# Waits for the loads of keys, queries and values put on attention's value matmuls, with gathers, low parts and one high part moved

## The chip, the core and the metric

The kernel runs on one core of a Trainium2 chip. The metric is the device time of one execution in microseconds (us). Before the change the median of three runs is 1334.23 us (1333.91 to 1335.32). TensorE does the matmuls, ScalarE the exponentials, VectorE and GpSimd the elementwise work, and SyncE issues most of the DMA loads and stores; each engine takes its instructions in the order of the program.

## What is computed

A gated mix of full attention and of a mixture of experts, for 2048 tokens of width 448, 16 heads of 28 and 8 experts of which each token uses two:

```python
def _A_ref(x, wqkv, wo):          # attention
    ...
    scores = jnp.einsum("bhqd,bhkd->bhqk", q, k) * scale
    p = _softmax(scores, axis=-1)
    o = jnp.einsum("bhqk,bhkd->bhqd", p, v)
    return (lambda x, *d: x.transpose(*d))(o, 0, 2, 1, 3).reshape(B, S, D) @ wo

def _B_ref(x, w_gate, w1, w2):    # experts
    ...
    for e in range(E):
        mask = (topk_idx == e)
        w = (gates * mask).sum(-1, keepdims=True)
        h = _silu(xf @ w1[e]) @ w2[e]
        out = out + w * h
    return out.reshape(B, S, D)

g = _sigmoid((x * gate_w).sum(-1, keepdims=True))
return g * _A_ref(x, A_wqkv, A_wo) + (1 - g) * _B_ref(x, B_w_gate, B_w1, B_w2)
```

## The kernel before

Matrix products keep their accuracy by splitting each float32 operand into a rounded high part and a low part (the rest); a product is then two or three matmuls. ScalarE, VectorE or GpSimd make the parts: a copy gives the high part, a subtraction the low part.

The program has four stages. First it projects x: tiles of x and pieces of the weight wv are split and multiplied into values, gate and logits (the split of wv is at L372 and L373, that of x at L390 and L392, the matmuls at L381); the tokens are sorted to the experts, and queries and keys are projected. Queries, keys (as high and low parts) and values go to DRAM. Second come the experts, to about 825 us, with the maxima of the scores beside them; each expert's rows are stored to DRAM (`ys_d`). Third is attention, 835 to 1292 us. Last, 16 tiles of the output projection.

Attention runs over 16 units; a unit is one group of four heads with 512 queries, u = 4 * group + quarter. Each unit has 8 pairs p of key tiles. The loop takes m = (u, p) in order; in each pass it issues the scores of the next pair (`score_passes`, L762: 24 matmuls in sets of four heads that run beside each other on four row groups), then the values of this pair (`values`, L1271: 32 matmuls into banks z0 and z1), then what lies beside (`beside`). The exponentials of a pair go to ScalarE (L1230, L1231, L1239, L1240). The last 160 columns of the eighth block are instead raised by `power`: GpSimd computes u (L1246), n (L1247) and g (L1248), then takes one entry of the list `due`, then computes e (L1251); VectorE turns g and e into P (L1253 to L1257). VectorE also copies scores out (X, L1232), accumulates the values (osb, L1279 and L1281) and divides by the row sums (`divide_half`, L1166, in pairs 2 and 3, by `rs`, which GpSimd's queue loads).

In `due` stand GpSimd's small DMAs: the row sums' way through DRAM, and the gathers of the experts' rows for the output tiles (`fetch_routed`, L1111: an indirect DMA from `ys_d` into b; the second of a tile adds). A gather is put there after pairs 4 and 6 of a unit.

The keys and values of a group are held in two halves of eight key tiles: K0 and V0 for pairs 0 to 3, K1 and V1 for pairs 4 to 7. In the last unit of a group, `beside` issues on SyncE the next group's K0 at pair 3, V0 at pair 4 and K1 at pair 6. `scores` issues the next unit's queries (Q) at pair 0. V1 is issued by `beside` at pair 0 of the new group's first unit, once its buffer is free. V1 is one DMA of 512 KB (L720); K0 and K1 are 12 DMAs each (L733, L736), Q is 12 (L748, L750). The matmul that first reads a loaded tile waits for its DMAs; where a matmul waits for several, TensorE gets a wait instruction more for each beyond the first.

In the last unit the first two output tiles are prepared: `split_o_high` at pairs 0 and 4, `split_o_low` (L186 and L187 in `split_xl`: low parts of three blocks, then of the half block) at pairs 2 and 7.

Of the kernel before, what the change touches and what calls it, by code (L numbers as in the profile page):

```python
# [9 lines left out]
F32 = mybir.dt.float32  # L10
# [41 lines left out]
KR = DH + 1  # L52
# [11 lines left out]
def tile_gated_mha_moe(ctx: ExitStack, tc: tile.TileContext, x, xe_, xT, wv, wqk, wo, w1, w2, out):  # L64
# [120 lines left out]
    def split_xl(pt, h, l, n):
        nc.vector.tensor_tensor(l, pt[:, 0:3, :n], h[:, 0:3].bitcast(F32), op=ALU.subtract)  # L186
        nc.vector.tensor_tensor(h[64:128, 3], pt[64:128, 3, :n], h[64:128, 3].bitcast(F32),  # L187
                                op=ALU.subtract)
# [98 lines left out]
    with ExitStack() as pa:  # L287
# [81 lines left out]
            split_x(xts[t].rearrange("p (b n) -> p b n", b=4), xh[:, :, ts], xl[:, :, ts], 128)  # L369

        def split_wv(b):
            nc.scalar.activation(wv_h[:, b], wv_r[:, b], AF.Copy)  # L372
# [15 lines left out]
        def split_xb(b, cs):  # L388
# [4 lines left out]
            else:  # L393
                nc.vector.tensor_tensor(xh[64:128, b, cs], xb[64:128], xh[64:128, b, cs].bitcast(F32),
                                        op=ALU.subtract)

        split_xb(0, slice(0, 128))
        split_wv(0)
        split_xb(0, slice(128, 512))
        for b in range(1, FIRST):  # L400
            split_xb(b, slice(0, 512))
# [313 lines left out]
    c0 = ctx.enter_context(tc.tile_pool(name="pc_sb0", bufs=1, side="right", reuse_waits="tile"))  # L715
    cpool = [c0, None]

    def load_v(g, hf):
        t = cpool[hf].tile([128, NT // 2, 128], F32, name=f"V{hf}")
        nc.sync.dma_start(t, v_d[hf * 1024:(hf + 1) * 1024, g * 128:(g + 1) * 128]  # L720
                          .rearrange("(t p) d -> p t d", p=128))
        return t


    def load_k(g, hf):
        r = []
        cs = slice(hf * 1024, (hf + 1) * 1024)
        for part, src in (("h", qkh_d), ("l", qkl_d)):
            kt_ = cpool[hf].tile([128, 1024], F32R, name=f"K{part}{hf}")
            kf = kt_.bitcast(F32)  # L730
            for j in range(4):
                r0 = D + (4 * g + j) * DH
                nc.sync.dma_start(kf[32 * j:32 * j + DH].rearrange("p (c n) -> p c n", c=2),  # L733
                                  src[2 * hf:2 * hf + 2, r0:r0 + DH].rearrange("c r n -> r c n"))
                if part == "h":
                    nc.sync.dma_start(kf[32 * j + DH:32 * j + KR], neg_d[:, cs])  # L736
            r.append(kt_)
        return r


    def load_q(g, qc):
        need_max(g, qc)
        q = c0.tile([128, 2, 512], F32R, name="Q", bufs=2)
        qf = q.bitcast(F32)
        for i, src in enumerate((qkh_d, qkl_d)):
            for j in range(4):
                r0 = (4 * g + j) * DH
                nc.sync.dma_start(qf[32 * j:32 * j + DH, i], src[qc, r0:r0 + DH])  # L748
        for j in range(4):
            nc.sync.dma_start(qf[32 * j + DH:32 * j + KR, 0], m_d[4 * g + qc, j:j + 1])  # L750
        return q

    Ps = {}
# [367 lines left out]
        else:  # L1121
            nc.vector.tensor_copy(oh, OT[:, :, t * 128:(t + 1) * 128])

    def split_o_low(t):
        split_xl(OT[:, :, t * 128:(t + 1) * 128], *halves[t], 128)

    def split_o(t, eng):
        split_o_high(t, eng)
# [70 lines left out]
    due = []  # L1199
# [18 lines left out]
    def scores(m):  # L1218
        u, p = divmod(m, NPR)
        if p == 0 and u and u + 1 < NU:  # L1220
            qs[u + 1] = load_q((u + 1) // 4, (u + 1) % 4)
        X = sb.tile([128, 512], F32, name="X")
        P = sb.tile([128, 8, 512], F32, name="P")
        z, t = [None] * 2, [None] * 2
        for i in range(2):
            kt = 2 * p + i
            z[i], t[i] = single(i), triple(i)
            three = [t[i][:, j] for j in range(3)]
            score_passes(kt, held[u // 4][0][kt // 8], qs[u], three + [z[i]] if i else [z[i]] + three)
        nc.scalar.activation(P[:, 0], z[0], AF.Exp, scale=SCALE)  # L1230
        nc.scalar.activation(P[:, 1:4], t[0], AF.Exp, scale=SCALE)  # L1231
        nc.vector.tensor_scalar(X, z[1], LAM * SCALE * math.log2(math.e), -126.0 * LAM, op0=ALU.mult, op1=ALU.max)  # L1232
# [6 lines left out]
        nc.scalar.activation(P[:, 4:7], t[1], AF.Exp, scale=SCALE)  # L1239
        nc.scalar.activation(P[:, 7, 0:512 - w], X[:, 0:512 - w], AF.Exp, scale=math.log(2.0) / LAM)  # L1240
        Pc[m] = [P[:, i] for i in range(8)]

    def power(x, to):
        u, n, g, y = (sb.tile([128, PW], F32, name=f"p{c}", bufs=1 + (c == "u")) for c in "ungy")
        e, v, w = u.bitcast(I32), x, g
        nc.gpsimd.tensor_scalar(u, x, 1.0 / LAM, ROUND, op0=ALU.mult, op1=ALU.add)  # L1246
        nc.gpsimd.tensor_scalar(n, u, -ROUND, LAM, op0=ALU.add, op1=ALU.mult)  # L1247
        nc.gpsimd.tensor_tensor(g, n, x, op=ALU.subtract)  # L1248
        if due:
            due.pop(0)()  # L1250
        nc.gpsimd.tensor_scalar(e, u, 127.0 - ROUND, 2.0 ** 23, op0=ALU.add, op1=ALU.mult)  # L1251
# [5 lines left out]
        nc.vector.scalar_tensor_tensor(to, w, EXP2[3], e.bitcast(F32), op0=ALU.add, op1=ALU.mult)  # L1257

    def values(m):
# [6 lines left out]
        for n, i in runs:  # L1266
            po, cs = parts[n]
            kt = 2 * p + i
            v = held[u // 4][1][kt // 8]
            for j in range(4):  # L1270
                nc.tensor.matmul(po[32 * j:32 * j + 32, cs], v[:, kt % 8, 32 * j:32 * j + 32], P[4 * i + j][:, cs],  # L1271
                                 start=i == 0, stop=i == 1)
# [14 lines left out]
    def beside(m):  # L1287
        u, p = divmod(m, NPR)
        g, qc = divmod(u, 4)
        if qc == 3 and g + 1 < NG:  # L1290
            if p == 3:
                held[g + 1] = [load_k(g + 1, 0), None], [None, None]
            if p == 4:
                held[g + 1][1][0] = load_v(g + 1, 0)
            if p == 6:
                held[g + 1][0][1] = load_k(g + 1, 1)
        if g and qc == 0 and p == 0:
            held[g][1][1] = load_v(g, 1)
# [18 lines left out]
        if u == NU - 1:  # L1317
            if p in (0, 4):
                split_o_high(p // 4, nc.vector)
            if p in (2, 7):  # L1320
                split_o_low(p // 7)

    for m in range(NU * NPR):
        if m + 1 < NU * NPR:
# [1 line left out]
        values(m)  # L1326
        u, p = divmod(m, NPR)
        if u + 1 < NU and p in (4, 6):
            due.append(lambda t=u + 1, c=p // 2 - 2: fetch_routed(t, c))
        if u == 0 and p in (0, 2):  # L1330
            due.append(lambda t=u, c=p // 2: fetch_routed(t, c))
        beside(m)
        if m + 1 in powers:
            next(powers[m + 1])
# [74 lines left out]
```

## Time and profile before

| | before |
|---|---|
| median of three runs | 1334.23 us |
| the profiled execution's own time | 1334.03 us |
| its span | 1332.2 us |
| TensorE busy | 1325.2 us |
| VectorE busy | 1064.0 us |
| GpSimd busy | 856.7 us |
| ScalarE busy | 843.5 us |
| granted TensorE clock | 1.00 |

The profile is of one execution. A row of a timeline has start and duration in us, the engine (PE is TensorE, PEld its weight loads, DVE VectorE, ACT ScalarE, POOL GpSimd, SPq SyncE's DMA queue), the line, the operation, out<-in and the number of instructions merged into it; in brackets stands an idle before it, with what ended it. A row of the windows has each engine's busy time in a stretch with the instructions in brackets, then the granted clock, the DMA engines' busy share and GB/s.

### The profile page before, as it was taken

The page shows a single profiled execution, that of the slowest core. Times are in us where ns is not written, and L with a number is a line of the kernel's source. Part 1 is how long each engine was busy: PE and PEld are TensorE (multiplying, and loading weights), DVE is VectorE, ACT ScalarE, POOL GpSimd, SP SyncE. Part 2 cuts the span into 40 slices and gives each one's busy share as a digit, 9 for nine tenths or more (in the row PEclk, how much of TensorE's full clock was granted, in tenths as well). Part 3 has the DMA queues.
Part 4 walks back from the last instruction along what each step waited for, and adds up shares of the span by engine and source line. Part 5 has one row for each costly group of instructions (what it writes and reads, how often), then busy time and mean ns, then how long its engine had stood idle before and what let it go on. Part 6 is the DMA issues. An engine that isn't in the chain of part 4 may idle for free. (4 is left out here: it accounts for less than half of the span.)

```text
span 1332.2 us, 32345 instructions
## 1 busy us (share of the span) xinstructions
PE 1325.2 (99%) x12210; PEld 936.9 (70%) x12210; DVE 1064.0 (80%) x1667; ACT 843.5 (63%) x1271; POOL 856.7 (64%) x1142
## 2 busy tenths in 40 slices
PE   9999999999999999999999999999999999999999
PEld 8888788788887777777777777555555555555558
DVE  5746899888898888989888786777788778777775
ACT  5325454355364344543445434999999999999981
POOL 2143967877787788786887844666666666656641
PEclk9999999999999999999999999999999999999999
DMA  9887657554553475455746423212422432242214
GB/s 349 301 268 267 185 162 187 153 151 109 166 157 86 149 203 149 137 125 155 187 120 184 93 78 68 62 39 64 121 54 70 113 81 49 76 111 54 49 41 137
DMA packets 139520, 176.83 MB, mean 133 GB/s; under 512 B 25576, under 2 KB 107242, under 8 KB 138850
## 3 DMA queue, kind: packets, MB, share of 16 engines
q1 hardware_dynamic: 120626, 145.68, 36.0%
q0 software_dynamic: 18592, 28.84, 10.5%
q8 instruction: 96, 1.57, 0.5%
q14 instruction: 62, 0.51, 0.1%
q10 hardware_dynamic: 144, 0.23, 0.1%
HBM read 124.54 MB, written 53.25 MB: 133 GB/s over the span
## 5 line engine op out<-in xcount | busy, mean ns | idle before, releaser
L149 DVE TENSOR_REDUCE mp<-pm 128x3 f32<-128x1536 f32 (+1 forms) x301 | 508.9, 1733 | 10.9 <-PE pm L128 10.8
L1271 PE MATMUL z<-P,V 128*32 128x288 f32 x4064 | 247.9, 382 | 1.0 <-ACT P L1230 0.2
L1271 PEld LDWEIGHTS z<-P,V 128*32 128x32 f32 x4064 | 110.2, 109 | 132.7 <-ACT P L1230 48.5
L1065 ACT ACTIVATE yo<-acc,cg 128x448 f32<-128x448 f32 x64 | 40.7, 636 | 232.1 <-PE acc L1050 222.7
L833 POOL TENSOR_TENSOR w2l<-w2r,w2h 128x448 fp32r<-128x448 f32 x112 | 130.6, 1167 | 86.1 <-ACT w2h L827 64.9
L762 PE MATMUL s<-Q,Kh 29*128 29x512 f32 x1524 | 185.7, 437 | 0.0
L1239 ACT ACTIVATE P<-s 128x1536 f32<-128x1536 f32 x127 | 185.4, 1460 | 0.0
L1231 ACT ACTIVATE P<-s 128x1536 f32<-128x1536 f32 x127 | 183.6, 1446 | 0.0
L762 PE MATMUL z<-Q,Kh 29*128 29x512 f32 x508 | 182.7, 438 | 0.0
L1050 PE MATMUL acc<-w2h,hh 128*128 128x448 f32 x448 | 167.0, 373 | 0.3 <-PEq L847 0.3
L1050 PE MATMUL acc<-w2h,hl 128*128 128x448 f32 x448 | 166.5, 372 | 0.0
L1050 PE MATMUL acc<-w2l,hh 128*128 128x448 f32 x448 | 166.1, 371 | 0.0
L997 ACT ACTIVATE hf<-acc 128x512 f32<-128x512 f32 (+6 forms) x154 | 74.3, 482 | 136.5 <-PE acc L993 130.6
L142 DVE TENSOR_REDUCE mp<-acc 128x1 f32<-128x512 f32 x130 | 89.5, 688 | 83.9 <-PE pm L128 81.8
L842 POOL TENSOR_TENSOR hl<-hf,hh 128x512 fp32r<-128x512 f32 x112 | 145.9, 1303 | 1.1 <-ACT hh L1000 0.5
L993 PE MATMUL acc<-xeh,w1h 128*128 128x512 f32 (+3 forms) x408 | 136.8, 339 | 0.0
L993 PE MATMUL acc<-xeh,w1l 128*128 128x512 f32 (+3 forms) x408 | 136.1, 338 | 0.0
L1246 POOL TENSOR_SCALAR pu<-X 128x160 f32<-128x160 f32 x126 | 44.4, 353 | 132.7 <-DVE X L1232 131.2
L1281 DVE TENSOR_TENSOR osb<-z,osb 128x288 f32<-128x288 f32 x224 | 95.1, 425 | 41.6 <-PE z L1271 31.9
L1232 DVE TENSOR_SCALAR X<-z 128x512 f32<-128x512 f32 x127 | 87.8, 691 | 44.5 <-PE z L762 30.8
L801 POOL TENSOR_TENSOR w1l<-w1r,w1h 128x1024 fp32r<-128x1024 f32 (+1 forms) x49 | 91.1, 1860 | 43.7 <-ACT w1h L795 24.2
L128 PE MATMUL pm<-khg,qg 28*128 28x512 f32 x894 | 110.5, 449 | 0.9 <-DVE lo L672 0.9
(238 smaller groups left out, 3072.4 us busy)
## 6 DMA issues: line engine op xcount, KB each, us to landing
w2r<-in_w_dram SPq DMA_DIRECT2D x112, 224.0 KB
w1r<-in_w_dram SPq DMA_DIRECT2D x56, 384.0 KB
x_d<-xf SPq DMA_DIRECT2D x115, 64.0 KB
ys_d<-zero_d SPq DMA_DIRECT2D x32, 224.0 KB
qkh_d<-hi SPq DMA_DIRECT2D x28, 256.0 KB
qkl_d<-lo SPq DMA_DIRECT2D x28, 256.0 KB
w1r<-in_w_dram SPq DMA_DIRECT2D x112, 64.0 KB
ys_d<-yo SPq DMA_DIRECT2D x32, 224.0 KB
```

Source lines behind the costliest of these rows:

```text
L128: nc.tensor.matmul(banks[n], qgs[g, qt // 4][rw, (qt % 4) * 128:(qt % 4 + 1) * 128], kh[g, kc][rw], start=True, stop=True)
L149: nc.vector.tensor_reduce(mp[:, (o + lo) % 256:(o + lo) % 256 + hi - lo], pm[h][:, lo - 3 * h:hi - 3 * h], axis=AX.X, op=ALU.max)
L762: nc.tensor.matmul(banks[j], k[rw, ks], q[rw, c], start=i == 0, stop=i == 2)
L801: nc.gpsimd.tensor_tensor(l[:, :, half], r[:, :, half], h[:, :, half].bitcast(F32), op=ALU.subtract)
L833: nc.gpsimd.tensor_tensor(w2l, w2r, w2h.bitcast(F32), op=ALU.subtract)
L842: nc.gpsimd.tensor_tensor(hl, hf32, hh[:, 0:512].bitcast(F32), op=ALU.subtract)
L993: nc.tensor.matmul(pu[:, 0:HC], a, b[:, cs], start=i == 0, stop=i == len(mms) - 1)
L1050: nc.tensor.matmul(py[:n, 0:D], a[:, cs], b, start=i == 0, stop=i == 3 * NH - 1)
L1231: nc.scalar.activation(P[:, 1:4], t[0], AF.Exp, scale=SCALE)
L1239: nc.scalar.activation(P[:, 4:7], t[1], AF.Exp, scale=SCALE)
L1271: nc.tensor.matmul(po[32 * j:32 * j + 32, cs], v[:, kt % 8, 32 * j:32 * j + 32], P[4 * i + j][:, cs], start=i == 0, stop=i == 1)
L1281: nc.vector.tensor_tensor(accs[u][:, cs], po[:, cs], accs[u][:, cs], op=ALU.add)
```

## The change

Four edits. (1) The gathers get a list of their own, `rows`, which is taken behind e instead of ahead of it. (2) In the last unit each low part is made in two pieces: the three blocks at pair 1 (first tile) and pair 5 (second), the half block at pairs 6 and 7. (3) The first high part of wv is copied by VectorE instead of ScalarE, and stands ahead of the first split of x. (4) The loads of K, Q and V are recorded, and `behind_values(u, p)` makes the value matmuls of pair (u, p) wait for those issued since the last such call, one DMA each, all but the first and the last of a block: Q at (u, 5), K0 at (u, 6), V0 at (u, 7), K1 at (u + 1, 1), V1 at (u, 2), where u is the unit that issues the load.

```diff
+            if b:
+                nc.scalar.activation(wv_h[:, b], wv_r[:, b], AF.Copy)
+            else:
+                nc.vector.tensor_copy(wv_h[:, b], wv_r[:, b])
...
+        split_wv(0)
         split_xb(0, slice(0, 128))
-        split_wv(0)
...
+    landing = []
+
+    def load(to, src):
+        landing.append(nc.sync.dma_start(to, src))
+
+    def landed():
+        r = landing[::-1]
+        landing.clear()
+        return r
...
+    def behind_values(u, p):
+        arrivals.setdefault(u * NPR + p, []).extend(landed())
...
             qs[u + 1] = load_q((u + 1) // 4, (u + 1) % 4)
+            behind_values(u, 5)
...
         nc.gpsimd.tensor_scalar(e, u, 127.0 - ROUND, 2.0 ** 23, op0=ALU.add, op1=ALU.mult)
+        if rows:
+            rows.pop(0)()
...
-                nc.tensor.matmul(po[32 * j:32 * j + 32, cs], v[:, kt % 8, 32 * j:32 * j + 32], P[4 * i + j][:, cs],
-                                 start=i == 0, stop=i == 1)
+                mm = nc.tensor.matmul(po[32 * j:32 * j + 32, cs], v[:, kt % 8, 32 * j:32 * j + 32],
+                                      P[4 * i + j][:, cs], start=i == 0, stop=i == 1)
+                if arrivals.get(m) and (i, j) not in ((0, 0), (1, 3)):
+                    tc.add_manual_dep(mm.ins, arrivals[m].pop(0).ins.name, DATA, reason="operands' arrival")
...
                 held[g + 1] = [load_k(g + 1, 0), None], [None, None]
+                behind_values(u, 6)
...
                 held[g + 1][1][0] = load_v(g + 1, 0)
+                behind_values(u, 7)
...
                 held[g + 1][0][1] = load_k(g + 1, 1)
+                behind_values(u + 1, 1)
         if g and qc == 0 and p == 0:
             held[g][1][1] = load_v(g, 1)
+            behind_values(u, 2)
...
-            if p in (2, 7):
-                split_o_low(p // 7)
+            if p in (1, 5):
+                split_o_low(p // 5, 0)
+            if p in (6, 7):
+                split_o_low(p - 6, 1)
...
-            due.append(lambda t=u + 1, c=p // 2 - 2: fetch_routed(t, c))
+            rows.append(lambda t=u + 1, c=p // 2 - 2: fetch_routed(t, c))
```

On TensorE, in unit 4, these are the value matmuls of pair 2 and the first scores of pair 4, which are the first to read K1; DMAHW3 and the like are semaphores of SyncE's loads. Before:

```order
L1271 MATMUL z0_12267<-P_12156,V0_11845 32x288 [waits Activation_49]
L1271 MATMUL z0_12267<-P_12156,V0_11845 32x288 x7
L1271 MATMUL z1_12268<-P_12156,V0_11845 32x224 [waits DVE_49]
L1271 MATMUL z1_12268<-P_12156,V0_11845 32x224 x6
L1271 MATMUL z1_12268<-P_12156,V0_11845 32x224 [waits DVE_49]
L762 MATMUL z0_12293<-Q_11406,Kh1_11985 128x512 [waits DMAHW4_49,DMAHW3_49,DVE_49]
L762 MATMUL s0_12294<-Q_11406,Kh1_11985 128x512 [waits DMAHW6_49,DMAHW5_49,Activation_49]
L762 MATMUL s0_12294<-Q_11406,Kh1_11985 128x512 [waits DMAHW7_49,DMAHW0_49]
L762 MATMUL s0_12294<-Q_11406,Kh1_11985 128x512 [waits DMAHW2_49,DMAHW1_49]
```

And after:

```order
L1296 MATMUL z0_12267<-P_12156,V0_11845 32x288 [waits Activation_49]
L1296 MATMUL z0_12267<-P_12156,V0_11845 32x288 [waits DMAHW3_49]
L1296 MATMUL z0_12267<-P_12156,V0_11845 32x288 x6
L1296 MATMUL z1_12268<-P_12156,V0_11845 32x224 [waits DVE_49]
L1296 MATMUL z1_12268<-P_12156,V0_11845 32x224 x6
L1296 MATMUL z1_12268<-P_12156,V0_11845 32x224 [waits DVE_49]
L776 MATMUL z0_12293<-Q_11406,Kh1_11985 128x512 [waits DVE_49]
L776 MATMUL s0_12294<-Q_11406,Kh1_11985 128x512 [waits Activation_49]
L776 MATMUL s0_12294<-Q_11406,Kh1_11985 128x512 x2
```

The scores have lost their waits for K1's DMAs, and the second value matmul of pair 2 has one for DMAHW3, which is V1's load.

Also on TensorE, two pairs later, the first matmuls that read V1. Before:

```order
L1271 MATMUL z0_12409<-P_12292,V1_12150 32x288 [waits DMAHW3_49,Activation_49]
L1271 MATMUL z0_12409<-P_12292,V1_12150 32x288 x7
L1271 MATMUL z1_12410<-P_12292,V1_12150 32x224 [waits DVE_49]
L1271 MATMUL z1_12410<-P_12292,V1_12150 32x224 x6
L1271 MATMUL z1_12410<-P_12292,V1_12150 32x224 [waits DVE_49]
```

And after:

```order
L1296 MATMUL z0_12409<-P_12292,V1_12150 32x288 [waits Activation_49]
L1296 MATMUL z0_12409<-P_12292,V1_12150 32x288 x7
L1296 MATMUL z1_12410<-P_12292,V1_12150 32x224 [waits DVE_49]
L1296 MATMUL z1_12410<-P_12292,V1_12150 32x224 x6
L1296 MATMUL z1_12410<-P_12292,V1_12150 32x224 [waits DVE_49]
```

The wait for DMAHW3 that stood here stands two pairs earlier now.

On GpSimd, one `power` with a gather in it. Before:

```order
L1247 TENSOR_SCALAR pn<-pu 128x160 [waits Pool_49]
L1248 TENSOR_TENSOR pg<-pn,X 128x160 [waits DVE_49,Pool_49]
L1111 DMA b_10187<-ys_d,slot_i 128x448 [waits DMASW7_49,DMASW0_49]
L1251 TENSOR_SCALAR pu<-pu 128x160
L1246 TENSOR_SCALAR pu<-X 128x160 [waits DVE_49]
```

And after:

```order
L1270 TENSOR_SCALAR pn<-pu 128x160 [waits Pool_49]
L1271 TENSOR_TENSOR pg<-pn,X 128x160 [waits DVE_49,Pool_49]
L1274 TENSOR_SCALAR pu<-pu 128x160
L1125 DMA b_10188<-ys_d,slot_i 128x448 [waits DMASW7_49,DMASW0_49]
L1269 TENSOR_SCALAR pu<-X 128x160 [waits DVE_49]
```

The gather has moved from ahead of e (the second line with pu<-pu) to behind it.

More of the change, by code (lines that the diff above doesn't have):

```diff
@@ L183, in split_x, with split_xl @@
         split_xl(pt, h, l, n)
[L185 to L188, printed above, removed]
+    def split_xl(pt, h, l, n, part=None):
+        if part != 1:
+            nc.vector.tensor_tensor(l, pt[:, 0:3, :n], h[:, 0:3].bitcast(F32), op=ALU.subtract)
+        if part != 0:
+            nc.vector.tensor_tensor(h[64:128, 3], pt[64:128, 3, :n], h[64:128, 3].bitcast(F32),
+                                    op=ALU.subtract)
     pe_cm = tc.tile_pool(name="pe_sb", bufs=1)
@@ L371, in split_wv @@
         def split_wv(b):
-            nc.scalar.activation(wv_h[:, b], wv_r[:, b], AF.Copy)
+            if b:
+                nc.scalar.activation(wv_h[:, b], wv_r[:, b], AF.Copy)
+            else:
+                nc.vector.tensor_copy(wv_h[:, b], wv_r[:, b])
             nc.vector.tensor_tensor(wv_l[:, b], wv_r[:, b], wv_h[:, b].bitcast(F32), op=ALU.subtract)
@@ L716, in tile_gated_mha_moe @@
     cpool = [c0, None]
+    landing = []
[5 more added lines that the diff above has]
+        return r
     def load_v(g, hf):
         t = cpool[hf].tile([128, NT // 2, 128], F32, name=f"V{hf}")
-        nc.sync.dma_start(t, v_d[hf * 1024:(hf + 1) * 1024, g * 128:(g + 1) * 128]
-                          .rearrange("(t p) d -> p t d", p=128))
+        load(t, v_d[hf * 1024:(hf + 1) * 1024, g * 128:(g + 1) * 128].rearrange("(t p) d -> p t d", p=128))
         return t
@@ L732, in load_k @@
                 r0 = D + (4 * g + j) * DH
-                nc.sync.dma_start(kf[32 * j:32 * j + DH].rearrange("p (c n) -> p c n", c=2),
-                                  src[2 * hf:2 * hf + 2, r0:r0 + DH].rearrange("c r n -> r c n"))
+                load(kf[32 * j:32 * j + DH].rearrange("p (c n) -> p c n", c=2),
+                     src[2 * hf:2 * hf + 2, r0:r0 + DH].rearrange("c r n -> r c n"))
                 if part == "h":
-                    nc.sync.dma_start(kf[32 * j + DH:32 * j + KR], neg_d[:, cs])
+                    load(kf[32 * j + DH:32 * j + KR], neg_d[:, cs])
             r.append(kt_)
@@ L747, in load_q @@
                 r0 = (4 * g + j) * DH
-                nc.sync.dma_start(qf[32 * j:32 * j + DH, i], src[qc, r0:r0 + DH])
+                load(qf[32 * j:32 * j + DH, i], src[qc, r0:r0 + DH])
         for j in range(4):
-            nc.sync.dma_start(qf[32 * j + DH:32 * j + KR, 0], m_d[4 * g + qc, j:j + 1])
+            load(qf[32 * j + DH:32 * j + KR, 0], m_d[4 * g + qc, j:j + 1])
         return q
@@ L1122, in split_o_high, with split_o_low @@
             nc.vector.tensor_copy(oh, OT[:, :, t * 128:(t + 1) * 128])
-    def split_o_low(t):
-        split_xl(OT[:, :, t * 128:(t + 1) * 128], *halves[t], 128)
+    def split_o_low(t, part=None):
+        split_xl(OT[:, :, t * 128:(t + 1) * 128], *halves[t], 128, part)
     def split_o(t, eng):
@@ L1198, in tile_gated_mha_moe @@
     powers = {}
-    due = []
+    due, rows = [], []
     NU = 4 * NG
@@ L1205, in tile_gated_mha_moe @@
     Pc = {0: Ps[0] + Ps[1]}
+    arrivals = {}
+    DATA = mybir.DependencyInfo(mybir.DependencyClass.Sync, mybir.DependencyReason.DATA)
+    def behind_values(u, p):
+        arrivals.setdefault(u * NPR + p, []).extend(landed())
+    landed()
     def single(i):
@@ L1328, in tile_gated_mha_moe @@
         if u + 1 < NU and p in (4, 6):
-            due.append(lambda t=u + 1, c=p // 2 - 2: fetch_routed(t, c))
+            rows.append(lambda t=u + 1, c=p // 2 - 2: fetch_routed(t, c))
         if u == 0 and p in (0, 2):
-            due.append(lambda t=u, c=p // 2: fetch_routed(t, c))
+            rows.append(lambda t=u, c=p // 2: fetch_routed(t, c))
         beside(m)
```

## The prediction

> **What bounds the kernel now.** I read the page's busy times first, then one quiet stretch of attention among the windows, then the timelines of ScalarE and TensorE there.
>
> ```profile
> span 1332.2 us, 32345 instructions
> PE 1325.2 (99%) x12210; PEld 936.9 (70%) x12210; DVE 1064.0 (80%) x1667; ACT 843.5 (63%) x1271; POOL 856.7 (64%) x1142
> ```
>
> Over the whole span TensorE is the one full engine. Parts 1, 2 and 4 of the change lie in attention (835 to 1292 us), part 3 at the start. The window's columns are TensorE, its weight loads, VectorE, ScalarE, GpSimd, granted clock, DMA share, GB/s.
>
> ```profile
> 985.00:1000.00 15.00, 15.00 (x240) 7.80 (x240) 12.58 (x34) 15.00 (x17) 8.29 (x18) 1.00 0.14 34
> ```
>
> Here two engines are full at once: TensorE 15.00 of 15.00 and ScalarE 15.00 of 15.00. VectorE has 2.42 us left in 4.2 iterations, 0.58 us in each. The iteration's length stands in ScalarE's timeline, between equal exponentials, and in TensorE's between equal blocks of value matmuls:
>
> ```profile
> 888.97 1.46 ACT L1239 ACTIVATE P<-s 128x1536 f32<-128x1536 f32 x1
> ...
> 892.54 1.46 ACT L1239 ACTIVATE P<-s 128x1536 f32<-128x1536 f32 x1
> ```
> ```profile
> 891.39 2.01 PE L1271 MATMUL z<-P,V 128*32 128x288 f32 x32
> ...
> 895.03 1.93 PE L1271 MATMUL z<-P,V 128*32 128x288 f32 x32
> ...
> 945.42 1.94 PE L1271 MATMUL z<-P,V 128*32 128x288 f32 x32
> ...
> 956.24 1.93 PE L1271 MATMUL z<-P,V 128*32 128x288 f32 x32
> ...
> 959.91 1.94 PE L1271 MATMUL z<-P,V 128*32 128x288 f32 x32
> ...
> 1071.37 1.93 PE L1271 MATMUL z<-P,V 128*32 128x288 f32 x32
> ...
> 1075.23 1.94 PE L1271 MATMUL z<-P,V 128*32 128x288 f32 x32
> ...
> 1186.96 1.93 PE L1271 MATMUL z<-P,V 128*32 128x288 f32 x32
> ...
> 1190.84 1.37 PE L1271 MATMUL z<-P,V 128*32 128x288 f32 x20
> ```
>
> ScalarE's iteration is 892.54 - 888.97 = 3.57 us. TensorE's with nothing in its way is 1.86 us of values (a block's printed length, less the tail that overlaps) and 1.7 us of scores, the same 3.56. With both full, neither can catch up: a stall of either is paid one for one. That is the rule that the rest goes by.
>
> **The new wait on V1.** The change gives each load that is issued ahead a value matmul that waits for it, and most of these are met early. For V1, the second half of the values, the place is early: the load is issued at pair 0 of the first unit of a group (units 4, 8 and 12), and the second value matmul of pair 2 of that unit waits for it, two pairs before any matmul reads V1. The rows above at 956.24, 1071.37 and 1186.96 are these pair 2 blocks. When V1 is there, the timeline of SyncE's queue and narrow windows tell:
>
> ```profile
> 936.25 0.48 SPq L720 DMA_DIRECT2D V<-v_d  x1
> ...
> 951.50 1.83 SPq L750 DMA_DIRECT2D Q<-m_d  x4
> 953.54 0.39 SPq L720 DMA_DIRECT2D V<-v_d  x1
> ...
> 1068.80 0.39 SPq L720 DMA_DIRECT2D V<-v_d  x1
> ...
> 1184.24 0.38 SPq L720 DMA_DIRECT2D V<-v_d  x1
> ```
> ```profile
> 958.00:959.00 1.00, 1.00 (x19) 0.85 (x16) 0.97 (x3) 1.00 (x2) 0.87 (x2) 1.00 0.07 17
> 959.00:960.00 1.00, 1.00 (x21) 0.64 (x20) 0.67 (x3) 1.00 (x3) 0.20 (x1) 1.00 0.00 0
> ...
> 1074.00:1075.00 1.00, 1.00 (x18) 0.67 (x12) 0.97 (x4) 1.00 (x3) 0.18 (x1) 1.00 0.03 8
> 1189.00:1190.00 1.00, 1.00 (x19) 0.86 (x19) 0.94 (x3) 1.00 (x3) 0.69 (x2) 1.00 0.20 52
> 1190.00:1191.00 1.00, 1.00 (x17) 0.58 (x17) 0.77 (x3) 1.00 (x2) 0.00 (x0) 1.00 0.00 0
> ```
>
> V1 is issued at 953.54, behind the pieces of K1 and of the next unit's queries; behind it only GpSimd sends 8 KB of row sums, so all but the last few KB of traffic is its own. The traffic ends in 958 to 959, 1074 to 1075 and the end of 1189 to 1190. I put the last bytes at 958.4, 1074.4 and 1190.0, and half a microsecond on top until the flag is seen: 958.9, 1074.9, 1190.5. That half is my choice; no row shows it, and 0 to 1 us bounds it. The waiting matmul is the second of its block, about 0.05 us after the block's start. The stalls:
>
> - unit 4: 958.9 - 956.3 = 2.6 us
> - unit 8: 1074.9 - 1071.4 = 3.5 us
> - unit 12: 1190.5 - 1187.0 = 3.5 us
>
> together 9.6 us (8.1 to 11.1 with the flag at its bounds). Behind the waiting matmul on TensorE stand the rest of that block, the scores of pair 4 and everything after; ScalarE, with pair 3's scores done, runs dry behind it. The Trainium skill says the same of the queue ("TensorE: Matmul & The Clock Gate", Part 2, Step-by-step): weight loads may be pulled ahead, the matmuls stay in program order; no row of the trace of before can show a matmul passing another.
>
> The other new waits I cost at nothing. V0 is issued at 936.25 and waited for behind 945.42 (pair 7 of unit 3), 9.2 us later, where V1 of the same size needs 5.4; K0 has three iterations (10.7 us), Q five (17.8). K1's pieces, issued from pair 6, are met at pair 1, just ahead of V1's place: what they cost, V1's stall swallows, since V1's landing is set by SyncE's queue and not by TensorE. For the same reason each gain in pairs 0 and 1 of units 4, 8 and 12 is lost.
>
> **What the moved waits give.** Before, the first score matmuls on new keys carried the waits, and each costs TensorE an instruction of its own. In the weight loads' timeline, an ordinary set of four row groups and one at a group's change:
>
> ```profile
> 939.93 0.19 PEld L762 LDWEIGHTS s<-Q,Kh 29*128 29x128 f32 x3
> ...
> 943.59 0.43 PEld L762 LDWEIGHTS s<-Q,Kh 29*128 29x128 f32 x3
> ```
>
> Three loads that started together (0.19 us) are spread over 0.43. At pair 0 of a group that is 0.2 us, swallowed as said. At pair 4, K1's first use, it lies behind the stall and is kept. The intervals from pair 2 to pair 3 are 959.91 - 956.24 = 3.67, 1075.23 - 1071.37 = 3.86 and 1190.84 - 1186.96 = 3.88; over 3.58 that is 0.09 + 0.28 + 0.30 = 0.67 us. Part of it may be something else that is late there, which a stall of 3 us covers as well. Gain 0.67 (0.3 to 0.7).
>
> **The gathers.** GpSimd's timeline where a gather stands before e, then VectorE's last step of the power, and its waits over 835 to 1292 us (total, times, longest):
>
> ```profile
> 889.60 0.53 POOL L1248 TENSOR_TENSOR pg<-pn,X 128x160 f32<-128x160 f32 x1
> 890.27 1.74 POOL L1111 DMA_INDIRECT b<-ys_d,slot_i  x1
> 892.09 0.33 POOL L1251 TENSOR_SCALAR pu<-pu 128x160 int32<-128x160 f32 x1
> ```
> ```profile
> DVE P L1257 <- POOL pu L1251: 2.5, 13, 0.2
> ```
>
> Without the gather ahead of it e is done by 890.5 instead of 892.4, and VectorE no longer waits; the 1.74 us stay on GpSimd, which has 6.71 of 15 us idle in the window above, and the next power's first step comes at 892.50 in any case. The price today is the interval 895.03 - 891.39 = 3.64 against 3.57, 0.07 us. Of 15 units, 12 keep the gain: at least 12 x 0.07 = 0.84; at most VectorE's waits, 12/15 of 2.5 = 2.0 (2.5 if all were kept). I take the middle, 1.4.
>
> **The last unit.**
>
> ```profile
> 1273.66 1.93 PE L1271 MATMUL z<-P,V 128*32 128x288 f32 x32
> ...
> 1277.24 1.18 PE L1271 MATMUL z<-P,V 128*32 128x288 f32 x16
> 1278.59 0.96 PE L1271 MATMUL z<-P,V 128*32 128x224 f32 x16 [0.17 <-DVE X L1232]
> ...
> 1281.18 2.19 PE L1271 MATMUL z<-P,V 128*32 128x288 f32 x32
> ...
> 1284.99 1.99 PE L1271 MATMUL z<-P,V 128*32 128x288 f32 x32
> ```
> ```profile
> 1276.00 0.55 DVE L186 TENSOR_TENSOR ol<-OT,oh 128x384 fp32r<-128x384 f32 x1
> 1276.56 0.29 DVE L187 TENSOR_TENSOR oh<-OT,oh 64x128 fp32r<-64x128 f32 x1
> ```
>
> The intervals are 3.58, 3.94 and 3.81: 0.36 + 0.23 = 0.59 us too long. The low part's 0.55 + 0.29 us stood in one iteration, over the 0.58 us that VectorE has left, and TensorE waited for X (0.17). Split over two, 0.55 fits barely. Gain 0.55 (0.2 to 0.6).
>
> **The start.**
>
> ```profile
> 4.27 0.57 ACT L372 ACTIVATE xeh<-wv_r 128x458 fp32r<-128x458 f32 x1
> ...
> 4.89 0.49 PE L381 MATMUL pq<-xeh,xh 128*128 128x458 f32 x1
> ```
>
> The first projection waits for this piece, which ScalarE makes behind a part of x. VectorE can make it beside that, but its own low parts then come later. I take 0.1, between a loss of 0.2 and a gain of 0.4.
>
> **Sum.** Against the profiled execution's own 1334.03 us (span 1332.2 and 1.8 around it; 0.2 below the median 1334.23): + 9.6 - 0.67 - 1.4 - 0.55 - 0.1 = + 6.9, so **1340.9 us**. Ends: 8.1 less gains of 3.6 (2.0 + 0.7 + 0.6 + 0.3) gives 1338.5; 11.1 less gains of 1.2 (0.84 + 0.3 + 0.2 - 0.1) gives 1343.9.
>
> **Rivals.**
>
> *V1 is there in time* (faster, 0.05). If the waiting matmul is met after V1 has landed, or is not waited for where the program says, only the gains stay, with all 15 gathers (1.75) and 0.2 at each of three group changes: 1334.03 - 3.7 = 1330.4. Against it: bytes still move at 958 while the block starts at 956.24, 1.7 us earlier. For it: that those bytes are V1's is inferred from the order of issue.
>
> *ScalarE's backlog pays for part* (within the bound, 0.05). When TensorE stops, ScalarE still has pair 3's exponentials. If TensorE could then run ahead by what it had waiting, some 1.5 us of each stall would come back: 9.6 - 4.5 - 2.7 = + 2.4, 1336.4. Against it: TensorE is at 15.00 of 15.00 too and has nothing to run faster with.
>
> *The clock falls after a stall* (slower still, 0.08). TensorE has not stood idle for as much as 3 us in attention before, so no row shows what its clock does then; all windows above say 1.00. If it ran one iteration at half speed after each of the two long stalls, each would cost up to 3.56 more: 1340.9 + 7.1 = 1348.0. The Trainium skill has such a rule ("TensorE: Matmul & The Clock Gate", Part 1, What's actually happening): after an idle window of about 3.4 us the clock goes to half until a busy window has passed. By it, as an estimate, each such stall costs 1.7 us on top. I give it little, since the stalls are hardly longer than that window.
>
> **Chances.** The forecast has 0.82; the rivals 0.05, 0.05 and 0.08, and the range from 1338.0 to 1344.0 leaves these out. Counting a change within 0.2% (2.7 us, about what a measurement of this kernel can tell) as none: faster 0.05, within 0.05, slower 0.90.
>
> **What would show it.** In the profile after, the value blocks of pair 2 in units 4, 8 and 12 should hold an idle of 2.6, 3.5 and 3.5 us on TensorE, put down to V1's load, with ScalarE idle shortly behind it; the interval at pair 3 and the one with a collecting gather should be near 3.57, and e should follow g without a gap. The prediction is wrong if these blocks run through, if the interval after a stall is shorter than 3.5 us (TensorE caught up), or if the window behind it shows a clock under 1.00.

## The result and the profile after

The changed kernel takes 1347.22 us (median of 6 runs, 1345.85 to 1351.29), the kernel before beside it 1334.27 (6 runs, 1333.57 to 1335.32). The ratio is 1.0101, 95% interval 1.009 to 1.0112: slower by 13 us, where the forecast was 1340.9 within 1338 to 1344. The direction was right, and so was the wait for V1; the forecast left out what the clock does behind that wait. The profiled execution took 1348.35 us, and its page begins:

```profile
span 1346.5 us, 32288 instructions
PE 1330.8 (99%) x12210; PEld 935.7 (69%) x12210; DVE 1064.8 (79%) x1668; ACT 841.4 (62%) x1270; POOL 858.2 (64%) x1142
```

The span has grown by 14.3 us. The busy times of VectorE, ScalarE and GpSimd changed by 0.8, -2.1 and 1.5 us. TensorE is busy 5.6 us more with the same number of matmuls: some of them ran slower. The rest it stood, and its waits (total, times, longest) say for what:

```profile
PE z L1296 <- DMA V<-v_d: 8.9, 3, 3.2
```

Before, this wait was not in the list. Its three places in TensorE's timeline of the changed kernel, the value blocks of pair 2 in units 4, 8 and 12:

```profile
957.60 0.67 PE L1296 MATMUL z<-P,V 128*32 128x288 f32 x2
961.22 1.93 PE L1296 MATMUL z<-P,V 128*32 128x288 f32 x30 [2.95 <-DMA V<-v_d]
...
1076.35 0.67 PE L1296 MATMUL z<-P,V 128*32 128x288 f32 x2
1079.84 3.28 PE L1296 MATMUL z<-P,V 128*32 128x288 f32 x30 [2.82 <-DMA V<-v_d]
...
1195.68 0.67 PE L1296 MATMUL z<-P,V 128*32 128x288 f32 x2
1199.51 3.63 PE L1296 MATMUL z<-P,V 128*32 128x288 f32 x30 [3.15 <-DMA V<-v_d]
1203.07 0.79 PE L776 MATMUL z<-Q,Kh 29*128 29x512 f32 x1
```

A matmul of a value block leaves two records, so a block of 32 records is 16 matmuls. Two records run (the first matmul), then nothing until V1 is there: 961.22 - 957.60 = 3.6, 3.5 and 3.8 us, together 10.9. (The bracket counts from the modelled end of the matmul before, so it is shorter.) Then look at the lengths. The other 30 records take 1.93 us in unit 4, as ever, but 3.28 in unit 8 and 3.63 in unit 12, and in unit 12 the first of the next scores take 0.79 us instead of 0.50. The windows of the changed kernel have the reason in the column behind the five engines:

```profile
956.34:959.75 3.41, 1.93 (x26) 0.69 (x18) 1.97 (x6) 3.41 (x5) 1.87 (x6) 1.00 0.75 200
1075.81:1079.22 3.41, 1.19 (x14) 0.22 (x6) 1.31 (x4) 3.41 (x4) 1.74 (x5) 1.00 0.55 130
1079.22:1082.63 3.41, 2.79 (x27) 1.55 (x30) 0.59 (x2) 0.14 (x1) 0.00 (x0) 0.50 0.00 0
1195.27:1198.69 3.42, 1.08 (x14) 0.18 (x6) 1.19 (x3) 3.40 (x4) 1.59 (x5) 1.00 0.71 177
1198.69:1202.10 3.41, 2.59 (x24) 1.41 (x27) 0.40 (x2) 0.00 (x0) 0.00 (x0) 0.50 0.01 1
1202.10:1205.51 3.41, 3.41 (x34) 2.02 (x27) 1.67 (x6) 0.71 (x2) 0.00 (x0) 0.50 0.01 2
```

The granted clock was 0.50 in the 3.41 us behind the second stall and in the 6.83 us behind the third, and 1.00 throughout behind the first. The rows of units 8 and 12 are cut where the clock changed; these places lie a multiple of 3.41 us apart, and the row of unit 4 is cut on the same grid. In the stretch ahead of a fall TensorE was busy 1.19 and 1.08 of 3.41 us; in unit 4 the stall lay across two such stretches, 1.93 us of the first and 1.95 of the second were busy, and the clock stayed. After the third stall one half-speed stretch was not enough: 2.59 of 3.41 us busy did not bring the clock back, 2.79 behind the second stall did. ScalarE, in the fourth group of numbers, runs dry behind the stall: 0.14 and 0.00.

What this costs: the blocks, from their first matmul to the next scores, are 3.61, 4.84 and 5.52 us longer than the usual 1.86, and the scores behind the third 1.0. That is 15.0 us, 10.9 of idle and 4.1 of half clock.

Attention as a whole, from the first scores of unit 0, pair 1, to those of the last pair, before and after:

```profile
825.94 0.74 PE L762 MATMUL pm<-Q,Kh 29*128 29x512 f32 x8
...
1286.92 0.50 PE L762 MATMUL z<-Q,Kh 29*128 29x512 f32 x1
```
```profile
827.49 0.50 PE L776 MATMUL pm<-Q,Kh 29*128 29x512 f32 x4
...
1301.24 0.50 PE L776 MATMUL z<-Q,Kh 29*128 29x512 f32 x1
```

It went from 460.98 to 473.75 us, 12.8 more. So against the 15.0 the moved steps gave 2.2 us. The other 1.55 us of the 14.3 came ahead of attention. One microsecond of that is in the first projections, which ran at the slow rate until 7.3 us (the tenth of them starts at 8.22 instead of 7.18). Their timeline, and part 3's copy on VectorE:

```profile
4.88 0.73 PE L386 MATMUL pq<-xeh,xh 128*128 128x458 f32 x1
...
6.95 0.59 PE L386 MATMUL pq<-xeh,xl 128*128 128x458 f32 x1
7.33 0.43 PE L386 MATMUL pq<-xel,xh 128*128 128x458 f32 x1
```
```profile
3.88 0.83 DVE L377 CAST xeh<-wv_r 128x458 fp32r<-128x458 f32 x1 [2.39 <-DMA wv_r<-in_wv_dram]
```

The copy took 0.83 us on VectorE (0.57 on ScalarE before), began as soon as the weights were there, and the first projection started when it did before, 4.88 against 4.89.

### The profile page after: what moved, and what is told of

It reads as the page before. It is cut to its first block, busy times and chain, and to the rows that moved or that the text cites. A ratio compares the mean times of both kernels' runs of the same rounds, so it can differ in the third digit from the quotient of the medians.

```text
span 1346.5 us, 32288 instructions
## 1 busy us (share of the span) xinstructions
PE 1330.8 (99%) x12210; PEld 935.7 (69%) x12210; DVE 1064.8 (79%) x1668; ACT 841.4 (62%) x1270; POOL 858.2 (64%) x1142
## 5 line engine op out<-in xcount | busy, mean ns | idle before, releaser
L149 DVE TENSOR_REDUCE mp<-pm 128x3 f32<-128x1536 f32 (+1 forms) x301 | 508.7, 1732 | 10.9 <-PE pm L128 10.8
L1296 PE MATMUL z<-P,V 128*32 128x288 f32 x4064 | 252.2, 386 | 9.5 <-DMA V<-v_d 8.9
```

What stands on the lines that cost most here:

```text
L149: nc.vector.tensor_reduce(mp[:, (o + lo) % 256:(o + lo) % 256 + hi - lo], pm[h][:, lo - 3 * h:hi - 3 * h], axis=AX.X, op=ALU.max)
L1296: mm = nc.tensor.matmul(po[32 * j:32 * j + 32, cs], v[:, kt % 8, 32 * j:32 * j + 32], P[4 * i + j][:, cs], start=i == 0, stop=i == 1)
```

## The experiments

Times are medians, ratios against the kernel before on the same chip. The runs came in three lots; on the chips of the first two the kernel before took 1334.2 us, on that of the third 1338.1.

**Without V1's wait.**

```diff
-            behind_values(u, 2)
+            landed()
```

> The changed kernel without one of its waits: the value matmuls of pair 2 no longer wait for V1, whose first reader waits for it again two pairs later; everything else of the change stays. Theory (the whole loss is V1's wait: 10.8 us of idle and some 4 us of half clock behind it): the three long value blocks at pair 2 have the usual 1.86 us, the clock stays 1.00 in attention, and the time is 1331 to 1333 us, below the kernel before. Rival (the other waits put on value matmuls, for K0, K1, V0 and Q, cost as well): 1335 us or more.

Measured: 1333.30 us, ratio 0.9994 (0.9985 to 1.0003). The windows around pair 2 of units 4, 8 and 12 in this run, whose blocks start at 956.87, 1072.29 and 1187.01:

```profile
955.00:960.00 5.00, 5.00 (x83) 2.67 (x79) 3.82 (x10) 5.00 (x7) 2.96 (x8) 1.00 0.55 153
1071.50:1076.50 5.00, 4.96 (x80) 2.72 (x76) 4.41 (x12) 4.88 (x7) 1.98 (x6) 1.00 0.36 86
1186.00:1191.00 5.00, 5.00 (x84) 2.62 (x80) 4.07 (x12) 5.00 (x8) 2.43 (x6) 1.00 0.38 103
```

TensorE is full but for 0.04 us, and the clock is 1.00. One line of the change costs 13.9 us (1347.22 - 1333.30), more than the whole difference. The rival falls, but the median lies above the 1331 to 1333 expected: without the wait the change cannot be told from none.

**V1's wait a pair later.**

```diff
-            behind_values(u, 2)
+            behind_values(u, 3)
```

> The changed kernel with V1's wait put on pair 3 instead of pair 2, 3.58 us later. Theory (the loss is V1's landing less the time at which the waiting matmul is reached): the stalls of 3.5 to 3.8 us shrink to 0 to 0.3 us each, the clock stays 1.00, and the time is 1331 to 1333.5 us, as without the wait. Rival (a wait on a value matmul is dear in itself wherever it stands, by the queue behind it): half of the loss or more stays, 1339 us or more.

Measured: 1334.08 us, 0.9997 (0.9988 to 1.0006). TensorE's waits no longer name V's load. 3.58 us later in the program, the wait costs nothing here, but the time is 0.6 us above the range. TensorE waited twice for VectorE at pair 4 instead (0.7 us together), whose division stood before its row sums had landed. That is taken up below. The place is not a safe one: V1's last packets end at 960.03, 1075.64 and 1190.82 in this trace, 0.96, 0.72 and 0.77 us ahead of the blocks of pair 3, and in the changed kernel 0.57 us passed between the last packet and the matmul. So by estimate 0.15 to 0.4 us are left, and in units 4 and 12 TensorE owes them to its own delay of 0.46 and 0.22 us.

**Work in place of the idle.** The waiting matmul is moved behind 21 matmuls that write to the same bank and are overwritten; with 9 in a second kernel.

```diff
+                if u and u % 4 == 0 and p == 2 and (n, i, j) == (0, 0, 1):
+                    for _ in range(7):
+                        for h in range(1, 4):
+                            nc.tensor.matmul(po[32 * h:32 * h + 32, cs], v[:, kt % 8, 32 * h:32 * h + 32],
+                                             P[4 * i + h][:, cs], start=True, stop=True)
                 mm = nc.tensor.matmul(po[32 * j:32 * j + 32, cs], ...
```

> The changed kernel with 21 matmuls more (7 sets of three, whose results are overwritten) ahead of the matmul that waits for V1, about 3.6 us of work in each of units 4, 8 and 12, so that TensorE works while it waits. V1 lands no earlier. Theory (the granted clock falls because of the idle): the clock stays 1.00, some 4 us come back, and the time is 1342 to 1344 us. Rival (what is over the 9.6 us forecast comes from elsewhere, later loads or a slower start): 1346 to 1349 us.

Measured with 7 sets: 1344.16 us (1343.04 to 1347.38), ratio 1.0075 (1.0061 to 1.0089), 0.16 us above the range expected. TensorE's timeline in unit 4 (L1299 is the added work, L1301 the values) and the windows behind the stalls of units 8 and 12:

```profile
957.85 3.33 PE L1299 MATMUL z<-P,V 128*32 128x288 f32 x39
961.58 1.74 PE L1301 MATMUL z<-P,V 128*32 128x288 f32 x27 [0.40 <-DMA V<-v_d]
```
```profile
1079.00:1083.00 4.00, 4.00 (x64) 2.56 (x62) 1.63 (x5) 0.75 (x2) 0.32 (x1) 1.00 0.02 5
1197.00:1203.00 6.00, 5.97 (x97) 3.54 (x95) 3.19 (x9) 2.69 (x5) 0.79 (x3) 1.00 0.01 3
```

V1 comes no earlier, nothing useful is done, and the kernel is 3.1 us faster than the changed one: the clock stays 1.00. This is the half clock, by itself. In the timeline the three blocks are 10.8 us longer than the usual 1.86 each: the added work costs what the idle did.

> The same with 9 matmuls more (3 sets of three), about 1.6 us of work, so that about 2 us of each idle stay. Theory (the clock falls only if the idle takes most of a counting window of 3.41 us): the clock stays 1.00 and the time is that of the run with 7 sets, 1342 to 1344 us. Rival (any idle of a microsecond or two is enough): the time stays at 1345 us or more, with a clock below 1.00 behind the stalls.

Measured with 3 sets: 1345.14 us (1342.49 to 1347.64), ratio 1.0076 (1.0062 to 1.009), granted clocks from 0.997 to 1.00. In the profiled run two stalls left the clock alone, and the third did not. The windows of the second and the third:

```profile
1074.13:1077.55 3.42, 2.34 (x32) 0.87 (x26) 1.47 (x4) 3.38 (x4) 1.84 (x6) 1.00 0.47 110
...
1193.59:1197.01 3.41, 1.38 (x20) 0.53 (x17) 0.65 (x2) 2.51 (x3) 1.50 (x4) 1.00 0.20 57
1197.01:1200.42 3.41, 3.41 (x34) 1.71 (x30) 0.87 (x3) 0.00 (x0) 0.00 (x0) 0.50 0.03 7
```
```profile
1196.80 3.48 PE L1301 MATMUL z<-P,V 128*32 128x288 f32 x30 [2.03 <-DMA V<-v_d]
```

An idle of 2.03 us was enough when it fell so that TensorE was busy only 1.38 of a 3.41 us stretch. The idle of unit 8 was longer, 2.08 us, but lay across two stretches with 2.34 and 2.38 us busy, and the clock stayed; it stayed in unit 4 too, with an idle of 1.61 us and 1.83 us busy in the stretch 958.07 to 961.49. So the condition of my theory held (2.03 of 3.41 us is more than half), but I had drawn the wrong forecast from it, that some 2 us of idle would never be most of a stretch; and the rival was too strong (two of three did nothing). Behind the stalls of the changed kernel and of this one the clock fell at 1.08, 1.19 and 1.38 us busy of 3.41, and stayed at 1.83, 1.93 and 2.34. The bound lies between 1.38 and 1.83. One more fall stands at the end of a program: in the trace of the last version without part 3 (below), the stretch from 1326.88 to 1330.30 has 1.60 us busy, and the clock is 0.50 behind it. A bound at half of the stretch, 1.71 us, fits all of these, but no run places it more closely. Where the stretches fall differs from run to run, which would explain, though no run shows it, why the changed kernel spreads over 5.4 us and the kernel before over 1.8: the slowest run, 1351.29 us, has the lowest mean clock (0.993), the fastest, 1345.85, the highest (0.997).

**V1's load ahead of the queries**, its wait kept at pair 2.

```diff
-        if p == 0 and u and u + 1 < NU:
+        if p == (u % 4 == 0) and u and u + 1 < NU:
             qs[u + 1] = load_q((u + 1) // 4, (u + 1) % 4)
...
                 behind_values(u + 1, 1)
+            if p == 7:
+                held[g + 1][1][1] = load_v(g + 1, 1)
+                behind_values(u + 1, 2)
-        if g and qc == 0 and p == 0:
-            held[g][1][1] = load_v(g, 1)
-            behind_values(u, 2)
```

> The changed kernel, all waits kept at their places, with the loads in another order: V1 is issued at the end of the unit before, ahead of the next queries instead of behind them, and in units 4, 8 and 12 these are issued one pair later. Theory (the loss is V1's landing less the time at which the waiting matmul is reached): V1 is issued some 5 us earlier, lands ahead of pair 2, the stalls and the half clock are gone, and the time is 1331.5 to 1334 us, as without the wait. Rival (the wait is dear in itself, or V1's load can't go earlier because SyncE's queue is full of K1's pieces): a stall of 1 us or more is left in each, 1337 us or more.

Measured: 1333.75 us, 0.9996 (0.9986 to 1.0005). SyncE's queue, TensorE's blocks of pairs 2 and 3 in unit 4, and VectorE's division between them:

```profile
949.38 0.39 SPq L726 DMA_DIRECT2D V<-v_d  x1
```
```profile
956.88 1.94 PE L1296 MATMUL z<-P,V 128*32 128x288 f32 x32
960.96 1.93 PE L1296 MATMUL z<-P,V 128*32 128x288 f32 x32
```
```profile
959.30 0.43 DVE L1180 TENSOR_TENSOR osb<-osb,rs 128x256 f32<-128x256 f32 x1 [0.71 <-DMA rs<-inv_d]
```

Issued 7.5 us ahead of the block instead of 2.4 (957.60 - 955.16 in the changed kernel), V1 is there, and the block runs through. A wait on a value matmul is free when its load has landed. The interval behind it is 4.08 us, though: again the division, which waited 0.71 us for its row sums.

**The parts alone.** Part 4 less V1's wait; part 1; part 3 (each put back on the kernel before, so the edits are those of the change).

> The kernel before with part 4 alone, less the wait for V1: K0, K1, V0 and Q are waited for by value matmuls, gathers, low parts and the start are as before. Theory (the late interval at K1's first use comes from VectorE's division, whose row sums land late, and not from the wait instructions): 0.26 us less at pair 0 of units 4, 8 and 12 and nothing else, attention 0.8 us shorter, 1333.4 us, with the intervals of pair 4 in units 8 and 12 still 0.2 to 0.3 us long. Rival (the step as forecast): these intervals fall to 3.58 too, another 0.67 us, 1332.8 us.

Measured: 1333.67 us, 0.9996 (0.9987 to 1.0005), above both values expected and not to be told from no change; attention 460.07 us in the profile, 0.91 less than before. Pair 0 of units 4, 8 and 12 is 0.20, 0.22 and 0.21 us shorter, as forecast; pair 4 is 0.10 and 0.30 shorter in units 4 and 8 and unchanged in unit 12. That is 0.40 of the 0.67 us forecast. The doubt that I put against the step expected no gain in units 8 and 12; it was wrong in the one and right in the other.

> The kernel before with part 1 alone: the gathers behind e instead of ahead of it. Theory (what it gives at one place it takes at another: the next u, n and g and the loads of the row sums start some 0.45 us later on GpSimd): about 0.1 us less in the iteration with a collecting gather, in 14 units, but 0.18 us more one iteration later in units 5 to 8, where VectorE also rounds wo, and longer waits for the row sums at pair 2; attention 0.3 to 0.8 us shorter, 1333.5 to 1334.0 us. Rival (the step as forecast): only the gain, 1.4 to 1.8 us, 1332.4 to 1332.9 us.

Measured: 1335.44 us, 1.0007 (0.9998 to 1.0016); attention 462.29 us, 1.3 longer. Here even the theory was too kind. VectorE's waits (total, times, longest), and VectorE and TensorE at pair 4 of unit 8:

```profile
DVE osb L1177 <- DMA rs<-inv_d: 2.5, 2, 1.8
```
```profile
1075.36 0.42 DVE L1177 TENSOR_TENSOR osb<-osb,rs 128x256 f32<-128x256 f32 x1 [1.77 <-DMA rs<-inv_d]
```
```profile
1076.14 0.50 PE L773 MATMUL z<-Q,Kh 29*128 29x512 f32 x1 [1.06 <-DVE osb L1305]
```

The division waited 1.77 us for the row sums, the accumulation behind it on VectorE came late, and TensorE, which needs that bank for the next scores, stood 1.06 us. GpSimd's timeline in this run shows where the row sums were held:

```profile
1064.15 1.79 POOL L1122 DMA_INDIRECT b<-ys_d,slot_i  x1 [0.27 <-issue]
1066.01 0.33 POOL L1266 TENSOR_SCALAR pu<-X 128x160 f32<-128x160 f32 x1
1066.42 0.33 POOL L1267 TENSOR_SCALAR pn<-pu 128x160 f32<-128x160 f32 x1
1066.83 0.53 POOL L1268 TENSOR_TENSOR pg<-pn,X 128x160 f32<-128x160 f32 x1
1067.30 0.77 POOL L1173 DMA_DIRECT2D rs<-inv_d  x1
```

Behind e, the gather pushes the next u, n and g and the load of the row sums, while e itself had time until the next X. The load's landing has no slack at pair 2.

> The kernel before with part 3 alone: wv's first high part by VectorE. Theory (the copy takes 0.83 us on VectorE there, against 0.57 on ScalarE, and delays the first low part of x, so that the first projections come later): attention begins 0.3 to 0.9 us later and the time is 1334.5 to 1335.2 us. Rival (the step as forecast; the late start in the changed kernel's profile was only the clock, which reached full speed at 7.4 instead of 4.9 us): 1334.0 to 1334.3 us.

Measured: 1334.40 us, 1.0001 (0.9991 to 1.001), between the two ranges: nothing that can be told from no change. Attention begins at 826.46 in its profile, and at 826.45 in that of part 4 alone, which has the old start. The late start of the changed kernel's profile was not part 3's. The slow first matmuls ended at 7.3 us there and at 5.2 us with the same part 3 and without V1's wait, in the timeline's lengths; with the old start at 6.6 in the profile of part 4 alone and at 7.3 in one of part 1 below, and with part 3 at 7.2 in that of V1 first.

Part 3 does leave a mark in attention, but one that nearly cancels. In the kernel before, ScalarE stood 0.22 us between two exponentials in unit 9, with no wait named that would explain it; with part 3 alone such a stop stands in unit 2 instead. The intervals there are 0.17 us shorter and 0.27 longer, and a like pair of differences is in every kernel with part 3 and in none without. Why ScalarE stops there stays open.

**The division later.** On the third chip: part 1 with the division at pairs 3 and 4; then V1 first with all parts and VectorE's steps moved; the same without part 3; the same without part 1.

```diff
-        if u > 1 and p in (2, 3):
-            divide_half(u - 2, p - 2)
+        if u > 1 and p in (3, 4):
+            divide_half(u - 2, p - 3)
...
-        if u > 1 and p == 3:
+        if u > 1 and p == 4:
             place(u - 2)
-        if p == 0 and 5 <= u < 9:
+        if p == 1 and 5 <= u < 9:
             split_wo_high(u - 5)
```

> Part 1 alone with the two halves of the division one pair later (pairs 3 and 4, the placing of the outputs at pair 4). Theory (part 1 alone is slower because GpSimd issues the row sums' load later and VectorE's division waits for it at pair 2): no wait of the division for its load in attention, the interval that was up to 1.28 us too long in unit 8 is 3.58, attention some 1.8 us shorter than with part 1 alone, 1333.5 to 1334.2 us. Rival (the loss of part 1 is elsewhere, as in units 5 to 8): 1335 us or more.

Measured: 1335.98 us, where the kernel before took 1338.08: 0.9983 (0.9973 to 0.9994). The absolute range expected does not apply on this chip. By the profile the theory holds, as far as profiles from different chips can be compared: the division no longer waits in the units (one wait of 0.7 us is left, that of the last unit), the interval in unit 8 is shorter than before by 0.19 us, and attention takes 460.60 us, 1.7 less than with part 1 alone.

> V1 issued ahead of the queries, all four parts, and three steps of VectorE moved away from those that are late: the division to pairs 3 and 4, the rounding of wo to pair 1 and its low halves to pairs 2 and 5, in the last unit the low part of the first tile to pair 2, the second tile's high part to pair 5 and low part to pairs 6 and 7. Theory (these are what took the gains of part 1 back): attention 2.5 to 3.2 us shorter than in the kernel before, 1331.5 to 1332.7 us. Rival (the late steps are set by GpSimd, not by what stands on VectorE): as with V1 first alone, 1333.5 us or more.

Measured: 1334.29 us, 0.9973 (0.9962 to 0.9985); attention 459.00 us, 2.0 less than in the profile of before: less than the 2.5 to 3.2 expected. In units 5 to 8 the 0.2 us of pair 1 are gone; two intervals in unit 2 are 0.28 and 0.39 us longer. The first is the one that every kernel with part 3 has; for the second I have no cause.

> The same without part 3 (wv's first high part by ScalarE as before). Theory (part 3 is worth nothing that can be measured): within 0.4 us of the run with it, 1331.5 to 1332.7 us. Rival (part 3 is worth some tenths of a microsecond, one way or the other): 0.5 us or more apart.

Measured: 1333.52 us, 0.9963 (0.995 to 0.9975); attention 458.54 us. It is 0.8 us from the run with part 3, more than the theory's 0.4, but with overlapping intervals, so part 3 stays undecided at that size. In its profile both long intervals of unit 2 are gone. This is the lowest ratio to a chip's own kernel before, 0.9963, where the changed kernel has 1.0101. On the chips of the first lots it was not run.

> The same with part 3 and without part 1 (gathers ahead of e as before). Theory (part 1 is worth 0.1 us in each of 14 units once what it delays is out of the way): 1.2 to 1.6 us longer than with it, attention 1.2 to 1.8 us shorter than before, 1332.7 to 1333.8 us. Rival (part 1 gives nothing): the same time as with it.

Measured: 1338.24 us, 0.9999 (0.9989 to 1.0009), 4 us behind the run with part 1, which is more than either theory said. In its profile the iteration with the first gather of a tile is 0.16 to 0.5 us longer in 13 of the units, 4.1 us over all. One of them, on TensorE and VectorE:

```profile
1089.01 1.18 PE L1294 MATMUL z<-P,V 128*32 128x288 f32 x16
1090.45 0.96 PE L1294 MATMUL z<-P,V 128*32 128x224 f32 x16 [0.26 <-DVE X L1255]
```
```profile
1089.70 0.69 DVE L1255 TENSOR_SCALAR X<-z 128x512 f32<-128x512 f32 x1 [0.50 <-PE z L776]
```

X begins late, though the scores before it end at 1089.1 and the profile names no wait of it for GpSimd, where the gather and e run beside it. Profiles from the other chips, gather ahead of e too, do not have this. So part 1 is worth about 4 us on this chip, and on the others no run shows such a gain. Why X is late there stays open. The kernel before, which has its gathers ahead of e too, is slower by 3.9 us on this chip (1338.08 against 1334.23); whether that is the same 4 us isn't shown, since it was timed on this chip but not traced.

## Why the prediction was wrong

The working against what was measured, in the profiled execution (+14.3 us, forecast +6.9):

| step | forecast | measured |
|---|---|---|
| V1's wait, idle | +9.6 | +10.9 |
| the clock behind the stalls | 0 | +4.1 |
| gathers, group's change, low parts | -2.6 | -2.2 |
| ahead of attention | -0.1 | +1.55 |

Of the 2.2 us in the third row 0.6 are gained at pair 0 of units 4, 8 and 12. The forecast had left these out, since the stall takes them back, and they are in its 10.9 us here. The sum's two ends took 0.3 and -0.1 us for the start where its text gives 0.4 and -0.2, which moves each end by 0.1 us.

**V1's wait** was right in place and mechanism, and 1.3 us short. V1 landed 6.1, 7.1 and 6.1 us after its issue (961.22 - 955.16 and so on), where I had taken 5.4, 6.1 and 6.3. The half microsecond of my choice was about right: in the trace V1's last packets end at 960.65, 1079.27 and 1198.95, and TensorE goes on 0.57, 0.57 and 0.56 us later. What I had wrong is the traffic beside V1, which I put at 8 KB. The queues in the trace of before, from 953 to 961 us (packets, MB, share of the DMA engines):

```profile
q1 hardware_dynamic: 1087, 0.58, 26.3%
q0 software_dynamic: 296, 0.27, 10.7%
```

The second is GpSimd's queue: the load of the row sums, 256 KB, issued 2.0 us ahead of V1 and still moving beside it. In unit 8 it was issued 2.1 us ahead of V1 before and only 1.0 us ahead in the changed kernel, and that is the unit where V1 took longest. With V1 issued first, none of that load moved beside V1, and the 512 KB took 2.2 to 2.4 us from the first packet to the last instead of 4.4 to 5.1. With the wait gone or free, the whole loss goes: shown by three runs.

**The clock** is the step that failed. I had it as a rival at 0.08, with "I give it little, since the stalls are hardly longer than that window". The clock under 1.00 behind a stall was also one of the signs that I had set for being wrong. My reasoning took it that an idle must fill a window. The measured falls came with 1.08 to 1.38 us of work left in the 3.41 us, so stalls of 3.5 to 3.8 us hit it two times in three, and one of 2.03 us did where one of 2.08 did not. With work in place of the idle the clock stayed: that it is the idle is shown by a run. The rival's own price, 1348.0, was close to the profiled 1348.35, partly by chance: it had two falls at 3.56 us each, and the profile has 1.35 and 2.7. The Trainium skill's rule ("TensorE: Matmul & The Clock Gate", Part 1, What's actually happening: half speed after an idle window of about 3.4 us, full speed after a busy one) is right on the length of the stretch, 3.41 us here, and on the half, 0.50; the estimate of 1.7 us for each stall that I drew from it lies between the 1.35 and the 2.7 measured. What idle means is the point where this case goes further: busy 1.38 of 3.41 us counted as idle, and 2.59 of 3.41 not yet as busy. The same page of the Trainium skill, in "HAM oscillation — how this bites in real kernels", describes waits for a transfer of 3 to 5 us that drop the clock at every tile; here two of three waits did. I should have weighed the rival by where the stall falls in the stretches, and not by its length alone.

**The moved waits** were right in two of three places: at pair 4 the intervals of units 4 and 8, less the stall, came out 0.10 and 0.30 us shorter in both the changed kernel and part 4 alone; that of unit 12 is 0.3 us shorter in the changed kernel and unchanged with part 4 alone. At pair 0, 0.2 us were lost to the stall as forecast (before it, they show in the timeline, and the stall takes them).

**The gathers** failed as a step. The gain at e is there, about 0.1 us in most iterations with a collecting gather, 1.2 us together with part 1 alone. (The changed kernel shows 1.45 in these places, but 0.27 of it is the interval in unit 9 that is shorter with part 3.) But 0.94 us comes back one pair later, most of it 0.17 to 0.19 in each of units 5 to 8, where VectorE rounds wo, and without V1's stall as cover the row sums land late for the division. Alone, part 1 lengthened attention by 1.3 us. I had looked at what waits for e and at GpSimd's idle share, not at what is queued behind the gather: the load of the row sums.

**The low parts** were right: 0.39 + 0.24 = 0.63 us against 0.55. Part 2 was not run alone; the two intervals are shorter by this in the changed kernel and in every kernel with it, and not in parts 1 and 4 alone.

**The start** was right as a term (nothing measurable), and wrong in this profile by something else: the first matmuls reached full speed some 2 us later. The profiles of the other kernels have that anywhere from 5.2 to 7.6 us, as late as 7.3 with the old start and as early as 5.2 with the new. 0.5 us more lies in stages that the change does not touch, and I did not find it. On the chips of the first two lots attention begins between 826.23 and 827.42 in the other kernels' profiles, so 827.49 is the end of a spread, and 825.94 in the kernel before the other end.

## What to carry to other kernels

Where two engines are full, put a wait for a load where the load has landed by the trace of that program. Here a wait one pair (3.58 us) too early cost its idle in full; one pair later it just held, and issuing the load earlier left room. Ask which other queue is moving when the load is. Price an idle of TensorE of 2 us or more with what the clock may take behind it. Before a slow instruction is moved behind another, read what stands next in that queue, and who waits for that.

## What the runs showed of the hardware that I had not expected

TensorE's clock fell to half behind stretches of 3.41 us in which it was busy 1.38 us or less, and 1.60 at the end of one program; it stayed at 1.83 us or more. After a fall a stretch with 2.59 us busy did not restore it while one with 2.79 did. A load of 512 KB took 2.2 to 2.4 us from first to last packet with next to nothing moving on GpSimd's queue, and 4.4 to 5.1 us beside most of a load of 256 KB. Filling an idle with matmuls that are thrown away made the kernel 3.1 us faster than leaving it idle. And the same program took 1338.1 us on one chip and 1334.2 on others, at a granted clock of 1.00 in most runs of both.
